# Second expert with seven block products for two of three token groups, and a planner that prices a shared port

## The chip, the cores and the metric

The kernel runs on one core of a Trainium2 chip. A core has five engines that run their own queues in order: TensorE (PE, matrix products into PSUM banks; PEld is its weight load), VectorE (DVE), ScalarE (ACT), GpSimd (POOL) and SyncE (SP, which starts DMAs). The metric is the device time of one execution in microseconds (us).

## The reference

Attention over 2 batches, 8 heads, 768 positions and head size 64, with a local window, a few global keys and a distance bias, then two feed-forward blocks on 1536 tokens of width 512:

```python
x = _attn_ref(q, k, v, n_global, n_local)   # as (1536, 512)
h = x @ moe_w_in                             # 512 x 2048
x = (h * sigmoid(h)) @ moe_w_out             # 2048 x 512
gate = sigmoid(x @ moe2_w_gate)              # 512 x 1536
val = x @ moe2_w_val                         # 512 x 1536
out = (gate * val) @ moe2_w_out              # 1536 x 512, result in float32
```

The weights arrive as 64-bit floats and are turned into 32-bit ones on the chip.

## The kernel before

Tokens are held feature-first, in three groups of 512 (`X[g]`). Every value of the two feed-forward blocks is kept as a high and a low half in TensorE's reduced fp32 format, and a product is three matmuls: high by high, high by low, low by high. All matmuls of the second block are 128 x 128 weights by 128 x 512 values.

A weight tile is 128 x 512 (512 KB in DRAM). `split_w` makes it from a staged load: one ScalarE op and three VectorE ops to reach 32 bits (`to_f32`), then one ScalarE op for the high half and one VectorE op for the low half. `pump_w` starts a load or a split every few units of work. There are 24 slots for finished tiles.

The program has two parts that are recorded and then reordered. The first is the attention, mixed with the first expert's front part. The second (`phase_rest`) runs tasks (phase, group, chunk of 128 hidden columns): `H` computes the hidden products, `act1`/`act2` apply the nonlinearity, `Y` multiplies by the output weights. In the second expert (phases B1 and B2, six chunks each, three groups) `H` makes a gate product and a val product, 12 matmuls each (4 slices of 128 input features, 3 matmuls each), and `Y` 12 more: 36 matmuls for a group and chunk, 1296 in all. Output sums stay in four PSUM banks over six chunks; `evac` then reads them once.

`Issue.order` sets the order on every engine: it walks over the recorded operations and always takes the one that can start first by its own price list (`Op.cost`, `SEM`, `TURN`), the earlier recorded where two are within 0.02. The instructions are issued in that order, and all of them carry line 257 in the profile, since one helper issues them. `nc`'s filler matmuls (line 1194, tile `warm`) stand where the planner sees room at the start. Names: `w` are weight tiles, `u` and `stage` their 32-bit form and raw load, `sg` and `g` a nonlinearity's value and its halves, `acc` the sums of a group, `x` the group's values, `t`, `pt`, `kt`, `ssum` and `nm_all` tiles of the attention.

Of the kernel before, what the change touches and what calls it, by code (L numbers as in the profile page):

```python
# [24 lines left out]
HA = 8  # L25
SLOTS = sum(r[-1] for r in PLAN)
NEG = 1.0e30
# [5 lines left out]
class Op:  # L33
# [20 lines left out]
    def cost(self):  # L54
        n = self.n
        self.form, self.half = None, 0
# [12 lines left out]
        elif self.eng == "vector":  # L69
# [3 lines left out]
            if self.meth == "tensor_scalar" and not psum and self.outs[0].name[0] == "t" and n > 64:  # L73
                self.occ += 0.1 + n / 1920.0
            self.lat = self.occ + 0.083
            self.locks = not psum and n > 128 and self.meth in ("tensor_tensor", "scalar_tensor_tensor")
        elif self.eng == "scalar":
            far = self.meth == "activation" and list(self.kw["in_"].ap)[-1][0] != 1
            slow = n > 256 and self.meth == "activation" and self.kw["in_"].space != PSUM
            self.occ = 0.045 + n / (960.0 if far else 1080.0 if slow else 1170.0) + (0.23 if "accum_out" in self.kw else 0.0)  # L80
            self.lat = self.occ + 0.1
        else:
            self.occ = n / 420.0 if self.meth == "tensor_tensor" and n > 256 else 0.13 + n / 790.0
            self.lat = self.occ + 0.03
# [20 lines left out]
def meets(x, y):  # L105
    if x[2] >= y[3] or y[2] >= x[3]:
# [6 lines left out]
        "rc": 0.195, "cr": 0.147, "tf": -0.082}  # L113


class Issue:


    def __init__(self, tc, nc):
        self.tc, self.nc, self.ops, self.on, self.open = tc, nc, [], False, None  # L120
        self.first, self.last, self.form, self.dq, self.filling = 0, {}, "f", 0.0, True
        self.lane, self.dve, self.busy = [0.0, 0.0], [], {}
        self.free, self.stop_fill = {e: 0.5 for e in SEM}, False
# [40 lines left out]
    def order(self, filler):  # L164
# [25 lines left out]
        while any(cand.values()):  # L190
            best = None
            for e, cs in cand.items():
                if cs:
                    at = [(max(free[e], max(max(m.ready, held(m)) for m in g)), p, i, g) for p, i, g in cs]
# [17 lines left out]
            for o in g:  # L212
# [9 lines left out]
                elif e == "gpsimd" and o.meth != "dma_start":  # L222
                    end = o.start + o.occ
                    for a, b in self.dve[-8:]:
                        if a < end and b > o.start:
                            end += b - max(a, o.start)
                    free[e] = end
                    o.lat = end - o.start + 0.03
# [5 lines left out]
                if e == "vector" and o.locks:  # L234
                    self.dve.append((o.start, free[e]))
# [26 lines left out]
class Engine:  # L262
# [3 lines left out]
    def __getattr__(self, meth):  # L266
        real = getattr(getattr(self.issue.nc, self.name), meth)

        def call(*args, **kw):
# [5 lines left out]
            o.stop_fill = iss.stop_fill  # L275
# [13 lines left out]
def attn_moe_moe2_kernel(  # L289
# [51 lines left out]
    clock = [0]  # L341

# [40 lines left out]
    halves2 = [range(0, C2 // 2), range(C2 // 2, C2)]  # L383
# [6 lines left out]
    for hh in halves2:  # L390
        for c in hh:
            add_w(("gate", c), colw(moe2_w_gate, c))
            add_w(("val", c), colw(moe2_w_val, c))
            add_w(("o2", c), roww(moe2_w_out, c))
# [3 lines left out]
    wtime = {}  # L398

    def wtile(key):  # L400
        return W[wid[key] % 24]

    def slot_free(n):
        if n < 16:
            return True
        if n < 24:
            return len(W) == 24
        return wfree[n - 24] >= 0
# [13 lines left out]
    def split_w(n):  # L422
        w = W[n % 24]
        st = next(u_r)
        to_f32(st, stages.pop(n))
        en.scalar.activation(out=w[:, 0, :], in_=st, func=AF.Copy)
        en.vector.tensor_tensor(w[:, 1, :], st, w[:, 0, :].bitcast(F32), ALU.subtract)

# [6 lines left out]
    def dma_w(n):  # L435
        st = next(stage_r)
# [4 lines left out]
    def pump_w():  # L441
# [3 lines left out]
        if n < wst["dma"] and clock[0] >= wtime[n] + wst["wait"] and clock[0] >= wst["last"] + wst["gap"]:  # L445
# [4 lines left out]
        if n < len(wsrc) and n - wst["split"] < 3 and slot_free(n):  # L450
# [3 lines left out]
    def need_w(key):  # L454
        n = wid[key]
        while wst["split"] <= n:
            m = wst["split"]
            if m >= wst["dma"]:
                assert slot_free(m)
                dma_w(m)  # L460
                wst["dma"] = m + 1
            split_w(m)
# [360 lines left out]
    def act2(tag, pg, pv):  # L823
        gt = next(g_r)
        g_t[tag] = gt
        sg = next(e_r)
        gf = sg
        en.scalar.activation(out=sg, in_=pg, func=AF.Sigmoid)

        def rest():  # L830
            en.vector.tensor_tensor(gf, sg, pv, ALU.mult)
            en.scalar.activation(out=gt[:, 0, :], in_=gf, func=AF.Copy)
            en.vector.tensor_tensor(gt[:, 1, :], gf, gt[:, 0, :].bitcast(F32), ALU.subtract)

        defer(4, rest)

# [94 lines left out]
    def phase_rest(prev):  # L931
        tasks = [("A1", NG - 1, c) for c in halves1[0]]
        tasks += [("A2", g, c) for g in range(NG) for c in halves1[1]]
        tasks += [("B1", g, c) for g in range(NG) for c in halves2[0]]
        tasks += [("B2", g, c) for g in range(NG) for c in halves2[1]]
        accs = acc + [main2["acc2"]]
        hi_ = [0]
# [3 lines left out]
        def H(ti):  # L941
            ph, g, c = tasks[ti]
            if ph[0] == "A":
                ps = bank[hi_[0] % 2]
                hi_[0] += 1
                for u in h_units(g, ("in", c), ps):
                    u()
                    unit()
                act1((ph, g, c), ps, False)
            else:  # L950
                pp = []
                for nm_ in ("gate", "val"):
                    ps = bank[hi_[0] % 4]
                    hi_[0] += 1
                    pp.append(ps)
                    for u in h_units(g, (nm_, c), ps):
                        u()
                        unit()
                act2((ph, g, c), pp[0], pp[1])

        def Y(ti):
            ph, g, c = tasks[ti]
            if ph[0] == "A":
                half, key, ring = halves1[0 if ph == "A1" else 1], ("out", c), [2, 3, 4, 5, 6, 7]
            else:
                half, key, ring = halves2[0 if ph == "B1" else 1], ("o2", c), [4, 5, 6, 7]
            first, last = c == half[0], c == half[-1]
            need_w(key)
            w = wtile(key)
            gt = g_t.pop((ph, g, c))  # L970
            if first:
                ybk["y"] = [bank[ring[(yrot[0] + d) % len(ring)]] for d in range(4)]
                yrot[0] += 4
            yb = ybk["y"]
            for d in range(4):
                sl = slice(d * 128, (d + 1) * 128)
                for a, b in ((0, 0), (0, 1), (1, 0)):
                    st = first and (a, b) == (0, 0)
                    fin = last and (a, b) == (1, 0)
                    if ph[0] == "A":  # L980
                        en.tensor.matmul(yb[d], w[:, a, sl], gt[:, b, :], start=st, stop=fin)
                    else:
                        en.tensor.matmul(yb[d], gt[:, a, sl], w[:, b, :], start=st, stop=fin)
                if last:
                    evac(ph, g, d, yb[d], accs[g])
                if d == 3 and g == NG - 1:
                    done_w(key)
                unit()

        def evac(ph, g, d, ps, ac):  # L990
            a = ac[:, d, :]
            if ph in ("A1", "B1"):
                en.vector.tensor_copy(a, ps)
            elif ph == "A2":
                en.vector.tensor_tensor(a, a, ps, ALU.add)
                en.scalar.activation(out=X[g][:, 0, d, :], in_=a, func=AF.Copy, scale=0.5)
                en.vector.scalar_tensor_tensor(
# [269 lines left out]
```

## Time and profile before

| | |
|---|---|
| median of 3 runs | 665.22 us (663.75 to 665.49) |
| the profiled execution | 663.89 us, its span 662.1 us |
| busy, share of the span | PE 98%, PEld 81%, DVE 56%, ACT 42%, POOL 13% |
| attention and start of the first expert | 0 to about 150 us |
| second expert | the last 1296 matmuls |
| end of PE | 655.6 us |

The busy share of PE alone doesn't say that it is at its peak, since matmuls overlap; what bounds a stretch is read from the waits and from how far apart matmuls start.

### The profile page before, as it was taken

How to read it: one execution, taken by the hardware profiler on the slowest of the kernel's cores; microseconds unless marked ns; L12 is line 12 of the kernel's file. 1: busy time of each engine (PE TensorE's matmuls, PEld its weight loads, DVE VectorE, ACT ScalarE, POOL GpSimd, SP SyncE). 2: the span in 40 equal slices, each digit the busy share in tenths (PEclk: the TensorE clock that was granted, in tenths of full speed). 3: DMA queues.
4: the chain of work that ended last, by engine and by line, in shares of the span. 5: the costliest groups of instructions: out<-in, count | busy, mean ns of one | idle time of the engine just before them, and what ended most of it. 6: DMA issues, size and time to landing. Idle time of an engine off the chain costs nothing.

```text
span 662.1 us, 9324 instructions
## 1 busy us (share of the span) xinstructions
PE 647.1 (98%) x3433; PEld 535.6 (81%) x3433; DVE 373.2 (56%) x869; ACT 277.2 (42%) x594; POOL 83.4 (13%) x167
## 2 busy tenths in 40 slices
PE   8799999999999999999999999999999999999996
PEld 6598888887888888888888888888888888888884
DVE  6999985555389999342799811312892212212212
ACT  4898787664346655222556411112452111111110
POOL 4355445333200000000000000000000000000000
PEclk9999999999999999999999999999999999999999
DMA  8757653001035545000145400000330000100101
GB/s 216 200 148 206 166 139 82 19 18 34 0 90 169 187 143 180 28 0 1 33 149 174 147 9 0 1 1 0 105 118 1 0 1 4 61 1 19 46 1 68
DMA packets 65301, 49.05 MB, mean 74 GB/s; under 512 B 39648, under 2 KB 60128, under 8 KB 65248
## 3 DMA queue, kind: packets, MB, share of 16 engines
q1 hardware_dynamic: 64032, 48.11, 25.1%
q8 instruction: 29, 0.48, 0.3%
q10 hardware_dynamic: 1216, 0.26, 0.2%
q14 instruction: 24, 0.20, 0.1%
HBM read 45.22 MB, written 3.15 MB: 73 GB/s over the span
## 4 chain that ended last, share of the span: by engine, by line
PE 86%; DVE 10%; issue 1%; ACT 1%; DMA 1%; POOL 0%; DVEq 0%; POOLq 0%
PE bank L257 86%; DVE u L257 3%; DVE t L257 2%; DVE acc L257 1%; DVE w L257 1%; ACT t L257 1%; DMA nraw<-in_n_local_dram 1%; DVE ssum L257 1%; DVE x L257 0%; DVE kt L257 0%; DVE sg L257 0%; ACT u L257 0%; DVE nm_all L257 0%; POOL t L257 0%; ACT pt L257 0%
## 5 line engine op out<-in xcount | busy, mean ns | idle before, releaser
L257 PE MATMUL bank<-x,w 128*128 128x512 f32 (+1 forms) x1488 | 349.1, 384 | 0.0
L257 PEld LDWEIGHTS bank<-x,w 128*128 128x128 f32 x1488 | 272.7, 188 | 53.5 <-issue 0.5
L257 PE MATMUL bank<-g,w 128*128 128x512 f32 (+1 forms) x624 | 145.0, 377 | 0.4 <-DVE acc L257 0.4
L257 PEld LDWEIGHTS bank<-g,w 128*128 128x128 f32 x624 | 110.7, 188 | 22.7 <-DVE acc L257 0.8
L257 ACT ACTIVATE sg<-bank 128x512 f32<-128x512 f32 x84 | 49.9, 595 | 158.7 <-PE bank L257 158.0
L257 DVE TENSOR_TENSOR sg<-sg,bank 128x512 f32<-128x512 f32 x36 | 24.7, 686 | 161.8 <-PE bank L257 161.8
L257 PE MATMUL bank<-w,g 128*128 128x512 f32 x432 | 103.4, 389 | 0.0
L257 ACT ACTIVATE g<-sg 128x512 fp32r<-128x512 f32 x84 | 53.1, 632 | 108.0 <-DVE sg L257 107.9
L257 DVE SCALAR_TENSOR_TENSOR u<-stage,u 128x512 int32<-128x512 int32 x136 | 95.0, 705 | 1.7
L257 PEld LDWEIGHTS bank<-w,g 128*128 128x128 f32 x432 | 81.1, 188 | 16.8
L257 DVE TENSOR_TENSOR g<-sg,g 128x512 fp32r<-128x512 f32 x68 | 46.8, 689 | 24.2 <-ACT g L257 23.7
L257 ACT ACTIVATE u<-stage 128x512 f32<-128x512 f32 x68 | 45.9, 676 | 32.8 <-DVE w L257 24.3
L257 ACT ACTIVATE w<-u 128x512 fp32r<-128x512 f32 x68 | 42.7, 630 | 32.5 <-DVE u L257 17.5
L257 POOL TENSOR_SCALAR t<-t,ssum 128x256 f32<-128x256 f32 (+1 forms) x88 | 48.6, 567 | 38.3 <-DVE ssum L257 35.0
L257 DVE SCALAR_TENSOR_TENSOR sg<-sg,bank 128x512 f32<-128x512 f32 x48 | 32.6, 681 | 36.6 <-ACT sg L257 36.6
L257 DVE TENSOR_TENSOR w<-u,w 128x512 fp32r<-128x512 f32 x68 | 46.7, 692 | 10.9 <-ACT w L257 10.7
L257 ACT ACTIVATE t<-t,nm_all 128x256 f32<-128x256 f32 (+1 forms) x96 | 45.8, 480 | 11.6 <-DVE nm_all L257 7.9
L257 DVE TENSOR_TENSOR acc<-acc,bank 128x512 f32<-128x512 f32 x48 | 32.1, 684 | 18.7 <-PE bank L257 18.6
L257 DVE CUSTOM_DVE_ANT_0 t<-bank,mask 128x256 f32<-128x256 f32 (+1 forms) x96 | 33.8, 393 | 5.9 <-PE bank L257 4.7
L257 DVE TENSOR_SCALAR u<-u 128x512 int32<-128x512 int32 x68 | 28.8, 426 | 4.2 <-ACT u L257 3.2
L257 ACT ACTIVATE pt<-bank 128x512 f32<-128x512 f32 (+1 forms) x48 | 26.0, 556 | 9.5 <-PE bank L257 9.3
L257 PE MATMUL bank<-ident,t 128*128 128x128 f32 x176 | 27.4, 277 | 2.3 <-POOL t L257 2.0
(68 smaller groups left out, 302.4 us busy)
## 6 DMA issues: line engine op xcount, KB each, us to landing
stage<-in_moe_w_out_dram SPq DMA_DIRECT2D x28, 512.0 KB, 3.5
stage<-in_moe_w_in_dram SPq DMA_DIRECT2D x16, 512.0 KB, 3.9
stage<-in_moe_w_gate_dram SPq DMA_DIRECT2D x12, 512.0 KB, 3.4
stage<-in_moe_w_val_dram SPq DMA_DIRECT2D x12, 512.0 KB, 3.6
v<-in_v_dram SPq DMA_DIRECT2D x12, 256.0 KB, 3.4
out_dram<-acc SPq DMA_DIRECT2D x12, 256.0 KB, 3.0
qk<-in_k_dram SPq DMA_DIRECT2D x11, 256.0 KB, 3.7
qk<-in_q_dram SPq DMA_DIRECT2D x11, 256.0 KB, 5.7
```

The costliest lines, as they stand in the source:

```text
L257: getattr(getattr(self.nc, o.eng), o.meth)(*o.args, **o.kw)
```

## The change

In the second expert chunks are taken in pairs, and groups 0 and 1 together. The input features are cut in two halves, so each of gate and val is, for a pair, a product of two 2 x 2 block matrices. These eight block products (6 matmuls each) become seven, after the scheme with seven products and fifteen block sums: four sums of value blocks (`X[1]`'s first half is overwritten by one; the others are `T2`, `T3`, `T4`), made once by GpSimd, ScalarE and VectorE when group 1 of the first expert is done; four sums of weight blocks for each pair and each of gate and val, made in `split` on VectorE (128 x 256 each), which fill two more weight tiles that ScalarE and VectorE halve; and sums of products, made by VectorE while it reads PSUM. Group 2 keeps plain products (`plain`). The output products (`down`) no longer stay in PSUM over six chunks: each pair gives a tile of 6 matmuls that ScalarE copies (first pair) or VectorE adds to `acc`, with banks 6 and 7 in turn.

Weight tiles have 16 slots in place of 24; in the second expert 12 of them serve tiles and four (4 to 7) the block sums. The price list: VectorE's tensor ops over 64 elements in SBUF now close a port shared with GpSimd, each of the two waits for the other in the plan, and `split` operations of the second expert are planned 0.5 later than they could start.

```diff
+SLACK = 0.5
...
-            if self.meth == "tensor_scalar" and not psum and self.outs[0].name[0] == "t" and n > 64:
-                self.occ += 0.1 + n / 1920.0
...
-            self.locks = not psum and n > 128 and self.meth in ("tensor_tensor", "scalar_tensor_tensor")
+            self.locks = not psum and n > 64 and self.meth != "tensor_reduce"
...
+            o.ready += o.slack
...
+        def shut(o, at):
+            a, b = self.port["gpsimd"]
+            return b if o.locks and a <= at < b else at
...
+                    a, b = self.port["vector"]
+                    got = max(o.start, b - 0.13) if a <= o.start < b else o.start
+                    free[e] = got + o.occ
...
+    loop2 = [0, 1, 2, 3, 8, 9, 10, 11, 12, 13, 14, 15]
+    slots += [loop2[n % 12] for n in range(len(wsrc) - NW1)]
...
+    SUMS = {"gate": (4, 5), "val": (6, 7)}
...
+        due = sums_due(n)
+        if due is not None:
+            a, b = ulast[0], st
+            le, ri = slice(0, 256), slice(256, 512)
+            en.vector.tensor_tensor(b[:, ri], b[:, le], b[:, ri], ALU.add)
+            en.vector.tensor_tensor(b[:, le], a[:, le], b[:, le], ALU.subtract)
+            en.vector.tensor_tensor(a[:, le], b[:, ri], a[:, le], ALU.subtract)
+            en.vector.tensor_tensor(a[:, ri], a[:, ri], a[:, le], ALU.subtract)
+            for f, sl in zip((b, a), SUMS[due[0]]):
+                en.scalar.activation(out=W[sl][:, 0, :], in_=f, func=AF.Copy)
+                en.vector.tensor_tensor(W[sl][:, 1, :], f, W[sl][:, 0, :].bitcast(F32), ALU.subtract)
...
+            if d < 2:
+                en.gpsimd.tensor_tensor(t, a, acc[0][:, d, :], ALU.subtract)
+                halved(lambda h: X[1][:, h, d, :], t)
             else:
...
+                en.gpsimd.tensor_tensor(t, a, t, ALU.subtract)
+                halved(lambda h: main2["T2"][:, h, j, :], t)
...
+        def product(ps, lhs, col, rhs, kk, start):
+            for j in range(2):
+                with en.together():
+                    for i, (a, b) in enumerate(((0, 0), (0, 1), (1, 0))):
+                        en.tensor.matmul(
+                            ps, lhs[:, a, col + j * 128:col + (j + 1) * 128], rhs[:, b, kk + j, :],
+                            start=start and j == 0 and i == 0, stop=j == 1 and i == 2, skip_group_check=not start,
+                        )
+                yield unit()
...
+            for i in range(2):
+                yield from product(bs[i][0], w[i][0], 0, X[0], 0, True)
+                en.scalar.activation(out=tc_[i], in_=bs[i][0], func=AF.Copy)
+            for i in range(2):
+                yield from product(bs[i][1], s[i][1], 0, T2, 0, True)
+                add(tu[i], tc_[i], bs[i][1])
+            for i in range(2):
+                yield from product(bs[i][2], s[i][0], 256, X[1], 0, True)
+            for i in range(2):
+                yield from product(bs[i][1], s[i][0], 0, T3, 0, False)
+                add(tv[i], tc_[i], bs[i][1])
+                add(tv[i], tv[i], bs[i][2])
...
+            for i in range(2):
+                yield from product(bs[i][1], w[i][1], 256, T4, 0, False)
+                add(tc_[i], tc_[i], bs[i][1])
...
+                yield from product(bs[i][2], s[i][1], 256, X[1], 2, False)
+                add(tu[i], tu[i], bs[i][2])
...
+                yield from product(bs[i][0], w[i][0], 256, X[0], 2, False)
...
+                a = accs[g][:, t, :]
+                if p == 0:
+                    en.scalar.activation(out=a, in_=yb, func=AF.Copy)
+                else:
+                    en.vector.tensor_tensor(a, a, yb, ALU.add)
```

Three places of the program show what moved. First TensorE in the second expert: before, two chunks of group 1 between output products (banks 2, 3, 0, 1 take gate and val; banks 4 to 7 the output sums).

```order
L257 MATMUL bank2_66<-x1_76,w11_94 128x512 x12
L257 MATMUL bank3_67<-x1_76,w12_95 128x512 x12
L257 MATMUL bank4_68<-w10_93,g2_106 128x512 x3
L257 MATMUL bank5_69<-w10_93,g2_106 128x512 x3
L257 MATMUL bank6_70<-w10_93,g2_106 128x512 x3
L257 MATMUL bank7_71<-w10_93,g2_106 128x512 x3
L257 MATMUL bank0_64<-x1_76,w14_97 128x512 x12
L257 MATMUL bank1_65<-x1_76,w15_98 128x512 x12
```

TensorE after, the end of the fourth pair's block products (banks 0 to 2 gate, 3 to 5 val; w4 to w7 are sums of weight blocks), then group 2's plain products.

```order
L260 MATMUL bank2_66<-x1_76,w4_87 128x512 x6
L260 MATMUL bank5_69<-x1_76,w6_89 128x512 x6
L260 MATMUL bank1_65<-t3_2064,w4_87 128x512 x6
L260 MATMUL bank4_68<-t3_2064,w6_89 128x512 x6
L260 MATMUL bank1_65<-t4_2065,w11_94 128x512 x6
L260 MATMUL bank4_68<-t4_2065,w13_96 128x512 x6
L260 MATMUL bank2_66<-x1_76,w5_88 128x512 x6
L260 MATMUL bank5_69<-x1_76,w7_90 128x512 x6
L260 MATMUL bank0_64<-x0_75,w10_93 128x512 x6
L260 MATMUL bank3_67<-x0_75,w12_95 128x512 x6
L260 MATMUL bank1_65<-x2_77,w10_93 128x512 x12
L260 MATMUL bank4_68<-x2_77,w12_95 128x512 x12
```

Runs of 12 matmuls into one bank became runs of 6, and a bank is written again after 6 matmuls into another one. Second, VectorE where output tiles are read: before, the sums of group 1 in the last phase.

```order
L257 TENSOR_TENSOR sg0_108<-sg0_108,bank1_65 128x512
L257 TENSOR_TENSOR acc1_79<-acc1_79,bank4_68 128x512
L257 TENSOR_TENSOR acc1_79<-acc1_79,bank5_69 128x512
L257 TENSOR_TENSOR g2_106<-sg0_108,g2_106 128x512
L257 TENSOR_TENSOR acc1_79<-acc1_79,bank6_70 128x512
L257 TENSOR_TENSOR acc1_79<-acc1_79,bank7_71 128x512
```

VectorE after, the third pair's output tiles of group 0 and the first of group 1 (`stage2` is the 32-bit form of the next weight tiles, in halves).

```order
L260 TENSOR_TENSOR acc0_78<-acc0_78,bank6_70 128x512
L260 SCALAR_TENSOR_TENSOR stage2_101<-stage0_99,stage2_101 128x512
L260 TENSOR_TENSOR acc0_78<-acc0_78,bank7_71 128x512
L260 SCALAR_TENSOR_TENSOR stage2_101<-stage0_99,stage2_101 128x512
L260 TENSOR_SCALAR stage2_101<-stage2_101 128x512
L260 TENSOR_TENSOR acc0_78<-acc0_78,bank6_70 128x512
L260 SCALAR_TENSOR_TENSOR stage2_101<-stage1_100,stage2_101 128x512
L260 TENSOR_TENSOR acc0_78<-acc0_78,bank7_71 128x512
L260 TENSOR_TENSOR g3_107<-sg0_108,g3_107 128x512
L260 TENSOR_TENSOR g2_106<-m3_2069,g2_106 128x512
L260 TENSOR_TENSOR acc1_79<-acc1_79,bank6_70 128x512
```

The reads of four banks stood together once in six chunks; now two banks alternate in every pair, and one to two operations of other work stand between two reads. Third, VectorE early in the attention (the first weight tile's low half `w0`, scores `t`, and group 0's low half `x0`): before.

```order
L257 TENSOR_TENSOR w0_83<-u0_102,w0_83 128x512
L257 ISA t4_137,nm_all_80<-bank0_64,mask0_113 128x256
L257 ISA nm_all_80 128x1
L257 TENSOR_TENSOR x0_75<-bank3_67,x0_75 128x4x128
L257 ISA t4_137,nm_all_80<-bank1_65,mask1_114 128x256
L257 ISA nm_all_80 128x1
```

The same place after.

```order
L260 ISA t4_137,nm_all_80<-bank0_64,mask0_113 128x256
L260 ISA nm_all_80 128x1
L260 TENSOR_TENSOR w0_83<-u0_102,w0_83 128x512
L260 ISA t4_137,nm_all_80<-bank1_65,mask1_114 128x256
L260 ISA nm_all_80 128x1
L260 ISA t0_133,nm_all_80<-bank0_64,mask0_113 128x256
L260 ISA nm_all_80 128x1
L260 TENSOR_TENSOR x0_75<-bank3_67,x0_75 128x4x128
```

Single operations changed places with neighbours; the same operations are there.

## Rows read from the trace of the kernel before

**Rows 1.** The page: span, and busy time of the engines.
```profile
span 662.1 us, 9324 instructions
PE 647.1 (98%) x3433; PEld 535.6 (81%) x3433; DVE 373.2 (56%) x869; ACT 277.2 (42%) x594; POOL 83.4 (13%) x167
```

**Rows 2.** The chain that ended last: start us, us, what.
```profile
86.46 59.70 PE bank L257 x433
...
152.87 500.68 PE bank L257 x2237
653.58 2.73 DVE acc L257 x4
```

**Rows 3.** All waits of TensorE: us in total, times, longest us.
```profile
PE bank L257 <- DVE x L257: 2.1, 4, 0.7
PE bank L257 <- POOL t L257: 2.0, 2, 1.9
PE bank L257 <- ACT kt L257: 1.8, 2, 1.4
...
PE bank L257 <- DVE acc L257: 0.4, 1, 0.4
```

**Rows 4.** Busy time by stretch (columns: length, engines busy, granted clock, DMA share, GB/s).
```profile
20.00:40.00 20.00, 16.32 (x149) 13.46 (x147) 19.49 (x65) 17.78 (x48) 8.07 (x17) 1.00 0.75 192
...
80.00:100.00 20.00, 19.82 (x162) 16.18 (x161) 17.73 (x69) 16.45 (x54) 10.23 (x20) 1.00 0.57 148
...
200.00:260.00 60.00, 60.00 (x266) 49.67 (x266) 59.06 (x106) 37.79 (x62) 0.00 (x0) 1.00 0.56 172
360.00:460.00 100.00, 100.00 (x443) 82.81 (x442) 33.95 (x55) 21.95 (x36) 0.00 (x0) 1.00 0.11 33
```

**Rows 5.** TensorE in order of time in the second expert: start us, us, what.
```profile
399.74 5.60 PE L257 MATMUL bank<-x,w 128*128 128x512 f32 x24
405.18 2.88 PE L257 MATMUL bank<-w,g 128*128 128x512 f32 x12
407.90 5.60 PE L257 MATMUL bank<-x,w 128*128 128x512 f32 x24
```

**Rows 6.** VectorE in order of time where it is full.
```profile
220.35 0.68 DVE L257 TENSOR_TENSOR g<-sg,g 128x512 fp32r<-128x512 f32 x1
220.96 0.42 DVE L257 TENSOR_SCALAR u<-u 128x512 int32<-128x512 int32 x1
...
222.02 0.42 DVE L257 TENSOR_SCALAR u<-u 128x512 int32<-128x512 int32 x1
222.35 2.01 DVE L257 SCALAR_TENSOR_TENSOR u<-stage,u 128x512 int32<-128x512 int32 x3
224.28 0.68 DVE L257 SCALAR_TENSOR_TENSOR sg<-sg,bank 128x512 f32<-128x512 f32 x1
```

**Rows 7.** VectorE and TensorE in order of time in the attention.
```profile
28.16 0.42 DVE L257 CUSTOM_DVE_ANT_0 t<-bank,mask 128x256 f32<-128x256 f32 x1
...
28.50 0.42 DVE L257 CUSTOM_DVE_ANT_0 t<-bank,mask 128x256 f32<-128x256 f32 x1
...
32.01 0.67 DVE L257 TENSOR_TENSOR x<-bank,x 128x512 fp32r<-128x512 f32 x1
...
32.74 0.44 PE L257 MATMUL bank<-ident,qk 128*128 128x128 f32 x2 [0.43 <-DVE x L257]
```

**Rows 8.** Costliest groups: mean ns of one ahead of the last bar.
```profile
L257 PE MATMUL bank<-w,g 128*128 128x512 f32 x432 | 103.4, 389 | 0.0
L257 ACT ACTIVATE u<-stage 128x512 f32<-128x512 f32 x68 | 45.9, 676 | 32.8 <-DVE w L257 24.3
L257 POOL TENSOR_TENSOR g<-sg,g 128x512 fp32r<-128x512 f32 x16 | 20.8, 1305 | 49.4 <-ACT g L257 42.0 <-issue 7.4
```

**Rows 9.** The end, in order of time.
```profile
647.26 8.32 PE L257 MATMUL bank<-w,g 128*128 128x512 f32 x36
...
653.58 2.73 DVE L257 TENSOR_TENSOR acc<-acc,bank 128x512 f32<-128x512 f32 x4 [3.97 <-PE bank L257]
654.33 2.34 SPq L257 DMA_DIRECT2D out_dram<-acc  x4
```

**Rows 10.** DMA issues: KB each, us to landing.
```profile
stage<-in_moe_w_val_dram SPq DMA_DIRECT2D x12, 512.0 KB, 3.6
```

More of the change, by code (lines that the diff above doesn't have):

```diff
@@ L222, in order @@
                 elif e == "gpsimd" and o.meth != "dma_start":
[L223 to L228, printed above, removed]
+                    a, b = self.port["vector"]
+                    got = max(o.start, b - 0.13) if a <= o.start < b else o.start
+                    free[e] = got + o.occ
+                    o.lat = free[e] - o.start + 0.03
+                    self.port[e] = got, free[e]
                 else:
@@ L233, in order @@
                     self.busy.setdefault(b, {})[e] = o.end
-                if e == "vector" and o.locks:
-                    self.dve.append((o.start, free[e]))
+                if o.locks:
+                    self.port[e] = o.start, free[e]
                 if o.meth == "dma_start":
@@ L341, in attn_moe_moe2_kernel @@
     clock = [0]
+    u_all, st_all = [next(u_r) for _ in range(2)], [next(stage_r) for _ in range(3)]
+    half2 = st_all[2].rearrange("p f t -> p (f t)").bitcast(F32)
+    u_all += [half2[:, 0:512], half2[:, 512:1024]]
     def run_due():
@@ L422, in split_w, with split @@
     def split_w(n):
-        w = W[n % 24]
-        st = next(u_r)
+        en.slack = SLACK if n >= NW1 else 0.0
+        split(n)
+        en.slack = 0.0
+    def split(n):
+        w = W[slots[n]]
+        st = next(u_r) if n < NW1 else u_all[n % 4]
         to_f32(st, stages.pop(n))
@@ L444, in pump_w @@
         n = wst["split"]
-        if n < wst["dma"] and clock[0] >= wtime[n] + wst["wait"] and clock[0] >= wst["last"] + wst["gap"]:
+        due = n < wst["dma"] and clock[0] >= wtime[n] + wst["wait"] and clock[0] >= wst["last"] + wst["gap"]
+        if due and can_split(n):
             split_w(n)
@@ L449, in pump_w @@
         n = wst["dma"]
-        if n < len(wsrc) and n - wst["split"] < 3 and slot_free(n):
+        if n < len(wsrc) and n - wst["split"] < (3 if n < NW1 else 2) and slot_free(n):
             dma_w(n)
@@ L941, in H @@
         def H(ti):
[L942 to L959, printed above, removed]
-        def Y(ti):
[L962 to L966, printed above, removed]
+            g, c = tasks[ti]
+            ps = bank[ti % 2]
+            for u in h_units(g, ("in", c), ps):
+                u()
+                unit()
+            act1((g, c), ps, False)
+        def Y(ti):
+            g, c = tasks[ti]
+            half = halves1[c >= HA]
             first, last = c == half[0], c == half[-1]
+            key = ("out", c)
             need_w(key)
             w = wtile(key)
-            gt = g_t.pop((ph, g, c))
+            gt = g_t.pop((g, c))
             if first:
-                ybk["y"] = [bank[ring[(yrot[0] + d) % len(ring)]] for d in range(4)]
+                ybk["y"] = [bank[(2, 5, 6, 7, 3, 4)[(yrot[0] + d) % 6]] for d in range(4)]
                 yrot[0] += 4
@@ L975, in Y @@
             for d in range(4):
[L976 to L983, printed above, removed]
+                mm3(yb[d], w, (slice(d * 128, (d + 1) * 128),), gt, (slice(0, G),), first, last)
@@ L1222, in attn_moe_moe2_kernel @@
         main2["acc2"] = late.tile([128, 4, 512], F32, name="acc2")
-        for n in range(16, 24):
-            W.append(late.tile([128, 2, 512], F32R, name=f"w{n}"))
+        for nm_ in ("T2", "T3", "T4"):
+            main2[nm_] = late.tile([128, 2, 2, 512], F32R, name=nm_.lower())
+        main2["M"] = [late.tile([128, 512], F32, name=f"m{i}") for i in range(5)] + [next(e_r), next(e_r)]
         wst["gap"] = 7
```

198 lines of the change are left out of this document (143 added, 55 removed).

## The prediction

> **What bounds the kernel now.** I read the page's first part, then the chain that ended last, then TensorE's waits, then the table by stretch. The page gives TensorE 98% of the span and VectorE 56% [rows 1], which alone proves little. The chain says more: but for a few us, all from 86 us to the end is TensorE's own matmuls, one piece of it 500.7 us with 2237 of them [rows 2]. TensorE's waits in the whole program come to about 7 us in the rows shown, nearly all in the attention, and its only wait for a sum of an expert is 0.4 us [rows 3]. From 200 to 260 us VectorE is busy 59.06 of 60.00 us and TensorE still 60.00 of 60.00, at granted clock 1.00 [rows 4]: a full VectorE costs TensorE nothing there, because nothing that TensorE needs soon stands behind it. In the second expert (360 to 460 us) VectorE has 34 of 100 us [rows 4]. So the second expert lasts as long as its matmuls take, and one matmul fewer is one less on the path, as long as VectorE and ScalarE keep up.
>
> What one matmul is worth: a period of 24 gate and val matmuls and 12 output matmuls runs from 399.74 to 407.90 us [rows 5], 8.16 us for 36, so 0.2267 us each, start to start. The mean duration of a record, 0.389 us [rows 8], contains 0.16 us in which the next already runs, and must not be multiplied.
>
> **The matmuls.** Before, a pair of chunks takes 2 x 3 groups x 36 = 216 matmuls. After, 7 block products x 6 matmuls for gate and as many for val make 84, group 2's plain products 2 x 24 = 48, the output products 3 groups x 4 tiles x 6 = 72: 204. Twelve fewer in each of six pairs are 72, and 72 x 0.2267 = 16.3 us. Attention and first expert keep theirs; two small filler matmuls more stand at the start, where TensorE has room. Forms are the same (128 x 128 by 128 x 512), so I keep 0.2267.
>
> **What VectorE gets.** Start to start, a 512-wide operation is 0.60 us (three in a row in 2.01 us, the next from 224.28) and a one-input one 0.34 (222.02 to 222.35) [rows 6]. The 256-wide two-input operation of the weight sums isn't in the trace: the nearest rows are the 256-wide scores, 0.34 apart (28.16, 28.50) [rows 7], and the 512-wide 0.60; I take 0.34, the same width, and 0.60 as the upper end. From one pair's first sum of products to the next pair's, the order after has 66, 77, 71, 70 and 51 VectorE instructions; with these prices 35.7, 41.3, 39.0, 38.4 and 29.0 us, against 204 x 0.2267 = 46.2 us of TensorE. At 0.60 for the narrow ones the fullest gets 12 x 0.26 = 3.1 us more, 44.4. So VectorE goes from a third to 77 to 90%, but isn't the longer of the two. ScalarE has 30 to 44 operations in a cycle, at most 0.68 us each [rows 8], 30 us: covered. GpSimd's eight new subtractions, 1.3 us each [rows 8], 10.4 us, lie beside group 2's part of the first expert, 192 matmuls or 43.5 us: covered, and if they were not, the first products with T2 would wait by what is left over.
>
> The duration of a 512-wide operation is 0.68 us in the rows while the next starts after 0.60 [rows 6]. The Trainium skill, "VectorE: DVE Perf Modes", section "The DRAIN you can't avoid", states that the next operation doesn't start until the pipeline is empty, though it allows an earlier start where nothing holds it. By the first half of that rule the fullest cycle would be priced with full durations, 58 wide operations at 0.68 and 19 narrow ones at 0.42, 47.4 us against TensorE's 46.2, and the sum would be 1.2 us higher; the trace bears out the second half, and I use starts.
>
> **What TensorE newly waits for.** The total fits, but not every bank does. Before, output sums are read once in six chunks, from four banks; after, tile by tile from banks 6 and 7 in turn, so that a bank is written again after six matmuls. The same holds inside a pair where a block product adds onto bank 1 or 4, which VectorE must have read first. How much time a read has: from the start of a tile's last matmul to the next start into that bank are 7 x 0.2267 = 1.59 us. It needs 0.39 for that matmul to end [rows 8], 0.04 to VectorE's start (matmul 27 of the last 36 starts at 647.26 + 26 x 0.2267 = 653.15, ends 653.54, VectorE starts 653.58 [rows 9]), 0.69 for the read (four that start 0.68 apart take 2.73 [rows 9]), and 0.06 until TensorE starts (VectorE ends 32.68, TensorE starts 32.74 [rows 7]): 1.18. So 0.41 us are left for what stands ahead in VectorE's queue. In a pair eight reads are this tight: six output tiles (the third to eighth wait for the first to sixth) and two block products; 48 in all.
>
> I laid the order of the third pair's tiles of group 0 along these numbers, tile ends 1.36 us apart. Reads start 0.20, 1.56, 3.10, 4.30 and 6.10 us after the first tile's sixth slot; the fifth tile could start at 4.08 and has its bank from 3.85. So the tightest has 0.23 us to spare, and no wait follows. The same in the fourth pair, where three matmuls of the next pair stand between tiles. Lower end: 0. Upper end: every one of the 48 finds a whole foreign operation ahead, 0.60 - 0.41 = 0.19 each, 9.1 us. A gain below 0 isn't there, since these waits don't exist now. I take one in ten late by this, 0.9 us, near the lower end, because the order written out shows none and the planner's matmul price, 0.0133 + 512/2400 = 0.2267, is what the trace shows.
>
> **Weights.** Sixteen slots in place of 24 mean that a pair's weight sums can be written only after the pair before has used its own. From that product (gate and val) until the next pair's first use, 12 + 48 + 48 = 108 matmuls follow, 24.5 us. The sums and four splits need 13.7 us of VectorE, its other work there 10.9: 24.6. That is just even, but the first two splits don't depend on it and stand earlier in the order; no wait, and 0.1 us a pair if they did. A load takes 3.6 us to land [rows 10], six in 46 us: hidden.
>
> **The attention.** The new port prices only swap neighbours there: at every eighth score the counts of splits, sums and groups done on VectorE before it are the same within one. TensorE's waits of that part, 2.1 for VectorE, 2.0 for GpSimd and 1.8 for ScalarE [rows 3], bound it: -2.0 if the wait for GpSimd goes, +2.0 if one like it comes. I take 0, since the counts agree.
>
> **The end.** The last read starts when TensorE ends (about 655.6 us) and the last DMA follows [rows 9]. After, output tiles come 1.36 us apart in place of 0.68, but the last read and last DMA stand equally far behind the last matmul: 0.
>
> **Sum**, in the profiled execution's own time: 663.89 - 16.3 + 0.9 = 648.5 us. The median of the runs shown is 665.22, which is 1.3 above; in its terms 649.8. I put the forecast between, 649.0.
>
> **Rivals.** (1) VectorE becomes a partner in step: every tight read meets one foreign operation, 9.1 us in place of 0.9, 656.7. For it: VectorE's queue is in order, filled to 90%, and some of its operations wait for ScalarE at its head. Against it: the order itself leaves 0.23 us at the tightest place. By the Trainium skill's full durations (the same section) one operation would cost 0.27 there, 13.0 us in all. (2) Slower than before: two foreign operations ahead of each tight read, because a weight split at the queue's head waits for ScalarE and reads pile up behind. Price (1.20 - 0.41) x 48 = 37.9 us, 685.5. It decides from 16.3 / 48 = 0.34 us lost at each read, that is 0.75 us of other work ahead of each. Against it: between two reads stand one or two operations, and the reads themselves are what VectorE has to do next. (3) The port prices matter: 646.5 where the attention loses its wait for GpSimd, 650.5 where it gains one more. That the change doesn't do what it says is out: the order has 72 matmuls less.
>
> **Chances.** Forecast, up to 651.5 us: 0.75. (1), 651.5 to 660: 0.14. (3) beyond 1.5 us: 0.08, half to each side. (2): 0.03. The range: 645.5 (profiled sum without waits, 647.6, less 2.0 for the attention) to 655.0, which takes in half of (1)'s waits on the upper terms; about 0.15 is left out. About 0.3%, 2 us, is what a measurement of this kernel can tell from no change; only a mixture of (1) and (2) ends there. Faster 0.95, same 0.02, slower 0.03.
>
> **What the profile after would show.** 1104 matmuls `bank<-x,w` and 216 `bank<-t,w`, in place of 1392, still 0.2267 us apart; TensorE's waits for `acc` and `m` operations under 1 us each and 2 us in all; VectorE at 75 to 90% in the second expert with no stretch of 20 us at 100%; the attention ending within 2 us of now. The forecast is wrong if matmuls of the second expert stand in runs of six with gaps, if TensorE waits for `acc` reads by 0.2 us and more again and again, if the granted clock falls, or if TensorE waits for `w` tiles at the start of a pair.

## The result, and the profile after

The changed kernel takes 646.40 us (median of 4 runs, 645.89 to 647.02), the kernel before 665.03 in the runs beside it (663.75 to 665.49): ratio 0.9723, 95% interval 0.9706 to 0.9741. The forecast was 649.0 with a range of 645.5 to 655.0. The profiled execution after took 646.85 us, its span is 645.1; before it was 663.89 and 662.1. Two executions of the kernel before beside later runs were slow, at a much lower clock (930.84 us at 0.655, 813.10 at 0.753), and enter no comparison.

The page after, answering to [rows 1]: span, and busy time of the engines. VectorE goes from 56 to 73%, TensorE's share is the same.

```profile
span 645.1 us, 9387 instructions
PE 634.1 (98%) x3363; PEld 523.5 (81%) x3363; DVE 470.8 (73%) x1043; ACT 307.5 (48%) x648; POOL 93.8 (15%) x175
```

The chain that ended last, answering to [rows 2] (start us, us, what). TensorE carries the chain from 152.71 until it ends at 639.2; before, it carried it from 152.87 to 653.55 and ended at 655.6, beside VectorE's last reads.

```profile
152.71 486.48 PE bank L260 x2174
639.21 0.69 DVE acc L260
```

All waits of TensorE, answering to [rows 3] (us in total, times, longest). None lies in the second expert; the wait for GpSimd's `t` went from 2.0 to 0.4 us, that for `x` from 2.1 to 0.5, while one for VectorE's `t` rose from 0.2 to 0.8.

```profile
PE bank L260 <- ACT kt L260: 1.8, 3, 0.9
...
PE bank L260 <- DVE t L260: 0.8, 1, 0.8
PE bank L260 <- DVE x L260: 0.5, 1, 0.5
PE bank L260 <- DVE acc L260: 0.4, 1, 0.4
PE bank L260 <- POOL t L260: 0.4, 1, 0.4
```

Busy time by stretch, answering to [rows 4], with the columns of those. From 360 to 460 us VectorE is now busy 86.18 of 100 us in place of 33.95, and TensorE still 100.00 of 100.00. New is the 0.91 of granted clock from 20 to 40 us, and that VectorE is busy 17.33 us with only 21 operations from 320 to 340 us, where GpSimd runs the eight subtractions.

```profile
20.00:40.00 20.00, 17.75 (x149) 14.78 (x147) 18.89 (x62) 17.66 (x48) 7.74 (x17) 0.91 0.67 180
...
320.00:340.00 20.00, 20.00 (x90) 16.57 (x89) 17.33 (x21) 11.66 (x20) 12.16 (x8) 1.00 0.00 1
360.00:460.00 100.00, 100.00 (x443) 82.84 (x442) 86.18 (x154) 48.86 (x83) 0.00 (x0) 1.00 0.27 81
```

A busy TensorE can still hide stalls: a matmul's record lasts 0.39 us and the next starts after 0.2267, so a stall below 0.16 us leaves no idle time. The sharper reading is how far apart the pairs start. The products with `t` tiles (`T2`, `T3`) come once in a pair; TensorE's rows of these, after:

```profile
369.61 5.60 PE L260 MATMUL bank<-t,w 128*128 128x512 f32 x24
...
415.85 4.24 PE L260 MATMUL bank<-t,w 128*128 128x512 f32 x18
...
462.09 5.60 PE L260 MATMUL bank<-t,w 128*128 128x512 f32 x24
...
508.33 5.60 PE L260 MATMUL bank<-t,w 128*128 128x512 f32 x24
...
554.57 5.60 PE L260 MATMUL bank<-t,w 128*128 128x512 f32 x24
...
600.87 5.60 PE L260 MATMUL bank<-t,w 128*128 128x512 f32 x24
```

The first five start 46.24 us apart, and 204 x 0.2267 = 46.24: the handovers between VectorE and TensorE cost 0.0 us there. The sixth starts 46.30 after the fifth, so 0.06 is lost once.

The other signs that the prediction named: its counts hold (1104 `x,w` and 216 `t,w` matmuls of 128x512), no stretch of 20 us in the second expert has VectorE over 18.71 us busy, and no wait is for a `w` tile. One sign of being wrong did show: the granted clock fell, but for 4 us in the attention and not in the second expert (last section).

### The profile page after: what moved, and what is told of

The parts are those of the page before. It is cut to its first block, busy times and chain, and to the rows that moved or that the text cites. A ratio compares the mean times of both kernels' runs of the same rounds, so it can differ in the third digit from the quotient of the medians.

```text
span 645.1 us, 9387 instructions
## 1 busy us (share of the span) xinstructions
PE 634.1 (98%) x3363; PEld 523.5 (81%) x3363; DVE 470.8 (73%) x1043; ACT 307.5 (48%) x648; POOL 93.8 (15%) x175
## 4 chain that ended last, share of the span: by engine, by line
PE 90%; DVE 6%; ACT 2%; issue 1%; POOL 1%; ACTq 0%; DVEq 0%
PE bank L260 89%; DVE u L260 2%; DVE t L260 1%; PE bank L1334 1%; DVE w L260 1%; POOL t L260 1%; ACT t L260 1%; DVE x L260 0%; DVE acc L260 0%; ACT kt L260 0%; DVE sg L260 0%; ACT u L260 0%; DVE ssum L260 0%; ACT pt L260 0%; DVE nm_all L260 0%
## 5 line engine op out<-in xcount | busy, mean ns | idle before, releaser
L260 PE MATMUL bank<-x,w 128*128 128x512 f32 (+1 forms) x1200 | 283.9, 383 | 0.0
L260 PEld LDWEIGHTS bank<-x,w 128*128 128x128 f32 x1200 | 218.4, 188 | 42.1 <-issue 0.5
L260 DVE TENSOR_TENSOR acc<-acc,bank 128x512 f32<-128x512 f32 x96 | 65.2, 684 | 31.2 <-PE bank L260 30.3
L260 DVE SCALAR_TENSOR_TENSOR u<-stage,u 128x512 int32<-128x512 int32 x100 | 69.2, 696 | 0.9
L260 ACT ACTIVATE g<-sg 128x512 fp32r<-128x512 f32 x60 | 37.9, 632 | 43.3 <-DVE sg L260 24.8
L260 PE MATMUL bank<-t,w 128*128 128x512 f32 x216 | 54.0, 389 | 0.0
L260 PEld LDWEIGHTS bank<-t,w 128*128 128x128 f32 x216 | 40.6, 188 | 8.4
L260 DVE TENSOR_TENSOR m<-m,bank 128x512 f32<-128x512 f32 x48 | 32.4, 683 | 17.0 <-PE bank L260 16.6
L260 DVE TENSOR_TENSOR g<-sg,g 128x512 fp32r<-128x512 f32 x44 | 31.0, 705 | 9.2 <-ACT g L260 7.8
L260 ACT ACTIVATE w<-stage 128x512 fp32r<-128x512 f32 x30 | 18.7, 628 | 32.0 <-DVE stage L260 19.9
```

Source lines behind the costliest of these rows:

```text
L260: getattr(getattr(self.nc, o.eng), o.meth)(*o.args, **o.kw)
```

## The experiments

Medians in us; "against" is the ratio to the kernel before as it ran beside them, with its interval. The kernel before was at 664.75, 664.39 and 664.79 beside runs 1 to 4, 5 to 8 and 9 to 11.

| run | what | median | against before |
|---|---|---|---|
| 1 | changed kernel, eight plain products for seven | 663.19 | 0.9975 (0.9964 to 0.9986) |
| 2 | changed kernel, old price list | 651.96 | 0.9804 (0.9790 to 0.9818) |
| 3 | kernel before, new price list alone | 663.40 | 0.9976 (0.9966 to 0.9986) |
| 4 | kernel before, last output tiles one by one | 663.74 | 0.9987 (0.9978 to 0.9996) |
| 5 | changed kernel, output tiles read twice | 649.43 | 0.9771 (0.9755 to 0.9786) |
| 6 | the same, read three times | 657.64 | 0.9894 (0.9878 to 0.9910) |
| 7 | changed kernel, no delay of splits | 647.89 | 0.9753 (0.9739 to 0.9767) |
| 8 | old price list, subtractions on VectorE | 648.48 | 0.9763 (0.9749 to 0.9777) |
| 9 | changed kernel again | 646.66 | 0.9723 (0.9709 to 0.9737) |
| 10 | run 7 again beside run 9 | 647.76 | 0.9741 (0.9727 to 0.9755) |
| 11 | new price list, subtractions on VectorE | 647.41 | 0.9740 (0.9725 to 0.9754) |

**1. Is it the number of matmuls?**

```diff
-                yield from product(bs[i][1], s[i][1], 0, T2, 0, True)
...
+            for g in (1, 0):
+                for j in (1, 0):
+                    for nm_, ps in (("gate", bank[k % 3]), ("val", bank[3 + k % 3])):
+                        for u in h_units(g, (nm_, 2 * p + j), ps):
```

> The changed kernel, but groups 0 and 1 take eight plain products for each pair of chunks (72 matmuls more, no block sums of weights or values); pairs, tile-by-tile output sums, sixteen slots and the new price list stay. Theory (the matmuls alone): 72 x 0.2267 = 16.3 us above the changed kernel's 646.4, so 662.7, within 1 us, TensorE without waits in the second expert. Rival (the new structure or the price list gave part of it): no more than 14 above, under 660.5. Rival (the block sums cost something that hides in the result): over 17.5 above, over 664.

It took 663.19, 16.8 above the changed kernel: nearly the whole gain goes when the 72 matmuls return, and 1.6 of 665 stay. The chain of run 1:

```profile
152.23 503.37 PE bank L260 x2246
```

Run 4 below, whose last tiles also come one by one, needs 502.72 us for as many matmuls. The 0.65 more of run 1 are handovers: its pairs of 216 matmuls start 48.97, 49.14, 49.16, 49.14 and 49.02 us apart, where 216 x 0.2267 = 48.96. TensorE's waits show none of them. So the step's size is read cleaner from run 4.

**2 and 3. The price list, taken back alone and made alone.**

```diff
-            self.locks = not psum and n > 64 and self.meth != "tensor_reduce"
+            self.locks = not psum and n > 128 and self.meth in ("tensor_tensor", "scalar_tensor_tensor")
...
-            a, b = self.port["gpsimd"]
-            return b if o.locks and a <= at < b else at
```

> The changed kernel planned with the old price list (port prices, costs and turn of before; the 0.5 of the weight splits stays). Theory (prices only swap neighbours): 646.4, within 1.5 us either way. Rival (the port prices shortened the attention): 648.5 or more, the attention ending 2 us later or more, with a wait of TensorE for GpSimd of about 2 us as in the kernel before.

> The kernel before, planned with the new price list and nothing else of the change. Theory (prices only swap neighbours): 665.0, within 1.5 us. Rival (the port prices shortened the attention): 663 or less, the last 1296 matmuls as they were and the attention shorter by 2 us.

Both runs swap the whole list: besides the port also the prices of some operations of GpSimd and VectorE and of one change of form on TensorE. Which of these moved the attention was not parted.

Run 3 is 1.35 us below the kernel before (interval 0.9 to 2.3), a number that its first theory's 1.5 us still takes in; the trace speaks for the rival: its attention ends earlier, at 151.38 in place of 152.87 in the chain, and of TensorE's waits that for `x` falls from 2.1 to 0.2 us, that for GpSimd's `t` from 2.0 to 1.6. The waits of run 3:

```profile
PE bank L259 <- POOL t L259: 1.6, 2, 1.3
...
PE bank L259 <- DVE x L259: 0.2, 1, 0.2
```

Run 2 lost 5.6 us, more than the attention can explain. TensorE's rows of run 2 at the second expert's start (idle time before a row in brackets) show where the rest is:

```profile
370.23 1.66 PE L259 MATMUL bank<-x,w 128*128 128x512 f32 x6 [2.14 <-DVE acc L259]
372.63 1.65 PE L259 MATMUL bank<-x,w 128*128 128x512 f32 x6 [0.73 <-DVE acc L259]
374.11 2.90 PE L259 MATMUL bank<-t,w 128*128 128x512 f32 x12
377.61 3.44 PE L259 MATMUL bank<-t,w 128*128 128x512 f32 x12 [0.60 <-DVE m L259]
```

And VectorE's rows of run 2 ahead of that:

```profile
365.14 0.42 DVE L259 TENSOR_TENSOR stage<-stage 128x256 f32<-128x256 f32 x1
367.61 0.43 DVE L259 TENSOR_SCALAR u<-u 128x512 int32<-128x512 int32 x1 [2.05 <-ACT u L259]
367.96 0.68 DVE L259 SCALAR_TENSOR_TENSOR u<-stage,u 128x512 int32<-128x512 int32 x1
...
369.49 0.68 DVE L259 TENSOR_TENSOR acc<-acc,bank 128x512 f32<-128x512 f32 x1
```

VectorE stands idle 2.05 us before a step of a weight split whose load (val) came later than the plan had it, and the `acc` read that TensorE needs stands behind it in the queue. Followed back, the chain of run 2 goes through that load (started at 361.43) and the gate load before it (351.57), each of which started 0.07 us after a step of VectorE on an earlier split, to VectorE from 322 us on. There VectorE's operations took up to 1.8 us in place of 0.68 beside GpSimd's subtractions:

```profile
327.42 3.48 DVE L259 SCALAR_TENSOR_TENSOR x<-acc,x 128x512 fp32r<-128x512 f32 x2
...
333.34 1.77 DVE L259 TENSOR_TENSOR w<-u,w 128x512 fp32r<-128x512 f32 x1
...
336.58 1.78 DVE L259 TENSOR_TENSOR w<-stage,w 128x512 fp32r<-128x512 f32 x1
```

The old list makes GpSimd wait for VectorE in the plan but never VectorE for GpSimd, so it planned these splits, and what follows them, too early. This was tested by runs 8 and 11.

**8 and 11. The same subtractions on VectorE, with either list.**

```diff
-                en.gpsimd.tensor_tensor(t, a, acc[0][:, d, :], ALU.subtract)
+                en.vector.tensor_tensor(t, a, acc[0][:, d, :], ALU.subtract)
```

(and the three lines like it)

> The changed kernel with the old price list, and the eight subtractions for the value sums on VectorE in place of GpSimd. With the old list alone it took 651.96, 5.6 above the changed kernel. Theory P (VectorE held up at the second expert's start, since GpSimd's subtractions use what both share): the loss there goes, only the attention's 1.4 stays: 647.8 within 1, TensorE without a gap from 360 to 380 us, VectorE's operations there 0.7 us each again. Rival (the old list spoils that place through the order alone, whoever subtracts): 651 to 653, gaps of TensorE at 370 to 380 us as with the old list.

> The changed kernel with its own price list, the eight subtractions on VectorE in place of GpSimd. With the old list this move was worth 3.5 us. Theory P (the new list already places GpSimd's subtractions where VectorE can bear them): nothing to win, 646.4 within 0.7. Rival (GpSimd's subtractions still cost VectorE time that TensorE feels): 1 us or more below. VectorE's operations between 320 and 340 us take 0.7 us each and not 1.2 to 1.8.

With the old list the move is worth 3.5 us (651.96 to 648.48), TensorE has no gap from 360 to 380 us (20.00 of 20.00), and its `t` products there start at 370.60, 1.0 later than after. So the loss comes with GpSimd's hold on VectorE where the plan takes it for nothing. The hold by itself costs TensorE nothing: in the kernel after VectorE is held as well (17.33 us for 21 operations, above), and the last val load starts no sooner (361.85 against run 2's 361.43), but the order of the new list puts the steps of both val splits behind the reads, from 370.71 on. Run 8's order differs from run 2's at this place too, so the two runs don't part the hold from the order that it spoils. With the new list there is nothing to win: 647.41, 0.75 above run 9. VectorE's operations from 320 to 340 us take 0.7 us each again in both runs. TensorE's row of run 8 shows what the move costs: here, where the first expert's products wait for a read of their bank behind VectorE's subtractions, some 0.7 us of the 1.0 arise; run 11 has the same wait:

```profile
335.11 3.01 PE L259 MATMUL bank<-x,w 128*128 128x512 f32 x12 [0.49 <-DVE sg L259]
```

**4. The end.** The kernel before, with the last two chunks of the last group multiplied tile by tile, so that the four sums are ready 1.36 us apart in place of 0.68.

```diff
+        def tail(left):
+            for d in range(4):
+                for ti in left:
...
+                evac("B2", g, d, ybk["y"][d], accs[g])
...
-            Y(ti)
+        tail(range(done, n))
```

> The kernel before, with the last two chunks of group 2 multiplied tile by tile, so that the last four output tiles come 1.36 us apart as in the changed kernel, in place of 0.68. Theory of the prediction (the last read and DMA stand equally far behind the last matmul): 665.0, no change. Rival (four DMAs at once cost the last one): the span ends 0.5 us sooner behind the last matmul (6.5 us before, 5.9 in the changed kernel), 664.5.

1.0 us below the kernel before (interval 0.3 to 1.5). The chain of run 4:

```profile
153.03 502.72 PE bank L257 x2246
655.77 0.69 DVE acc L257
```

The span ends 5.85 us behind TensorE, against 6.5 before (662.1 - 655.6) and 5.9 after (645.1 - 639.2). The difference is the last DMA itself: it starts 0.76 us behind TensorE's end in both (656.34 before, 656.49 in run 4), and lands 3.9 us later before and 3.3 in run 4, where the four stand further apart. That they get in each other's way is the likely reading; nothing else was tried. The row of the chain also gives the matmuls' price with the same kind of end: 502.72 - 486.48 = 16.24 us for 2246 - 2174 = 72.

**5 and 6. How much the handover bears.**

```diff
+                    for _ in range(1 if g < 2 else 0):
+                        en.vector.scalar_tensor_tensor(out=a, in0=yb, scalar=0.0, in1=a, op0=ALU.mult, op1=ALU.add)
```

(two in run 6)

> The changed kernel, where VectorE reads every output tile of groups 0 and 1 a second time in pairs 2 to 6 (one 512-wide operation more ahead of the bank's release; the output stays the same). 0.60 us more make the tight handover 1.18 + 0.60 = 1.78 us against 1.59, and 30 of them (6 in each of 5 pairs) are in the program. Theory A, the handover is what decides, with the sizes of the prediction: 0.19 x 30 = 5.7 us or more above the changed kernel's 646.4, so 652 to 656, with TensorE's waits for acc reads of 0.1 to 0.3 us each in the second expert, again and again. Theory B, only VectorE's total counts, and 8 more operations of 0.60 fill its fullest cycle to 46.1 of 46.2 us: 646.4, no waits.

> The same with two more reads of each tile. Theory A: handover 2.38 against 1.59 us, 0.79 x 30 = 23.7 us above the changed kernel, about 670, TensorE waiting for acc reads by 0.8 us each. Theory B (totals): VectorE's cycles 45.3, 50.9, 48.6, 48.0 and 38.6 against 46.2 us, 4.7 + 2.4 + 1.8 = 8.9 us above, about 655.

Run 5 lies between the theories, 3.0 us above the changed kernel. Its pairs start 46.24, 46.39, 46.38, 46.37 and 46.37 us apart, so they lose only 0.14 each: the planner, which knows of the second read, put three matmuls into another bank between output tiles (rows of 6 `w,g` with 3 `x,w` or `t,w` between them from 483.98 us; after, 30 and 18 `w,g` stand together). Only the last pair, where nothing is left to put between, shows theory A. Its end in the chain of run 5:

```profile
631.70 1.67 PE bank L260 x6
633.40 0.70 DVE acc L260
634.12 0.70 DVE acc L260
634.87 1.67 PE bank L260 x6
...
638.03 4.40 PE bank L260 x18
```

Two tiles in 3.17 us, 0.22 a tile more than 1.36, where 0.19 was worked out; from its first `w,g` (623.10) to TensorE's end 2.8 us are lost. Run 6, 11.2 us above, is nearer to theory B's 8.9 than to A's 23.7, but its parts are not B's. From its first `t` product (370.33) to its last 72 `w,g` matmuls (627.17) it loses 3.8 us against after (369.61 to 622.63), with VectorE busy 97.68 of 100 us from 500 to 600; and 6.9 more in the last pair, where B expected nothing, since its last tiles come every 2.04 to 2.14 us: three reads take VectorE 0.72 + 0.72 + 0.60 = 2.04. TensorE's rows of run 6 there:

```profile
627.17 2.88 PE L260 MATMUL bank<-w,g 128*128 128x512 f32 x12
630.93 1.66 PE L260 MATMUL bank<-w,g 128*128 128x512 f32 x6 [0.87 <-DVE acc L260]
632.97 1.67 PE L260 MATMUL bank<-w,g 128*128 128x512 f32 x6 [0.39 <-DVE acc L260]
635.11 1.63 PE L260 MATMUL bank<-w,g 128*128 128x512 f32 x6 [0.47 <-DVE acc L260]
...
646.19 4.37 PE L260 MATMUL bank<-w,g 128*128 128x512 f32 x18 [0.33 <-DVE acc L260]
```

**7, 9 and 10. The delay of the splits.**

```diff
-SLACK = 0.5
+SLACK = 0.0
```

> The changed kernel with the weight splits of the second expert planned without the 0.5 of delay (SLACK = 0.0). Theory A: the 0.41 us that a tight handover leaves, 0.23 at the tightest place, are enough in either order: 646.4 within 1 us, no wait of TensorE in the second expert. Rival: the delay is what keeps splits out of the way of reads; without it single reads stand behind one operation more, 0.2 to 0.6 us each, 5 to 20 times: 648 to 655 with waits for acc or m operations.

> The changed kernel again, beside the next two on the same chip, so that differences of 1 to 2 us can be told: 646.4 within 0.7, first sum products of a pair (24 matmuls on t tiles) 46.24 us apart, which is 204 x 0.2267.

> The changed kernel without the delay of the splits, again, beside the changed kernel. If the 1.5 us that it took longer are its own (its pairs lasted 46.46 to 46.70 us in place of 46.24), it is 1.1 to 1.8 above the changed kernel here too; if they were the chip's, within 0.5 of it.

Theory A is wrong by a little: 647.76 against 646.66 side by side, 1.1 us more, and 1.5 in run 7. The rival's mechanism is there, at the small end of its price. The list of waits shows none of it; the start of the pairs does, 46.42 to 46.48 us apart in run 10 (46.46 to 46.70 in run 7) in place of 46.24, which run 9 shows again (46.33 the last time). VectorE's rows of run 10 in the fourth pair show how one such 0.15 us arises:

```profile
509.82 0.69 DVE L260 TENSOR_TENSOR m<-m,bank 128x512 f32<-128x512 f32 x1 [3.39 <-PE bank L260]
510.42 0.69 DVE L260 TENSOR_TENSOR w<-u,w 128x512 fp32r<-128x512 f32 x1
511.02 0.69 DVE L260 TENSOR_TENSOR m<-m,bank 128x512 f32<-128x512 f32 x1
```

After, the two reads at this place stand back to back:

```profile
509.89 1.41 DVE L260 TENSOR_TENSOR m<-m,bank 128x512 f32<-128x512 f32 x2 [2.14 <-PE bank L260]
```

Without the delay a split's step is taken between two reads, the second is 0.60 late, and the 24 `t` products last 5.76 us in place of 5.60. That is most of the 0.2 that a pair loses, and about the price worked out for one foreign operation ahead of a tight read, 0.60 - 0.41 = 0.19, measured as 0.15.

## Why the prediction was right, and where its terms were off

**The matmuls** (16.3 us): right. 16.24 us from run 4 against after, and a pair of 46.24 us. Run 1 takes the 72 matmuls back and loses 16.8, 0.65 of it by its own handovers.

**The handovers** (0.9, between 0 and 9.1): the lower end held, 0.0 in four distances of pairs and 0.06 in the fifth. Rival (1) named a real mechanism with about the right price for one operation (0.15 to 0.22 measured, 0.19 expected), but it hardly occurs in the changed kernel: operations do stand between reads, but the order with its delay of 0.5 puts them where a read has the time. It costs 1.1 us without the delay and, with it, 0.65 in run 1, not 9.1. Rival (2) didn't come near in any run: even two more reads of each tile cost 11.2 us.

**VectorE's load**: right, 86.18 of 100 us from 360 to 460, and no cycle longer than TensorE's. From pair to pair it was busy 38.2, 41.6, 40.2, 39.9 and 28.6 us (its busy time between the starts above), where 35.7, 41.3, 39.0, 38.4 and 29.0 were worked out. One reading was wrong: the three operations from 222.35 to the next at 224.28 [rows 6] are 1.93 us, 0.64 each and not 0.60, since one of them needs the result of the one ahead and starts 0.72 us after it. The price of 0.60 stands in another of these rows (220.35 to 220.96). The full durations that the Trainium skill, "VectorE: DVE Perf Modes", section "The DRAIN you can't avoid", names first would have made a pair 47.4 us, as the prediction worked out. It is 46.24. Where an operation does need the one ahead, as run 5's second read of a tile, the next start came after 0.72 us (633.40, 634.12), not 0.60; there the rule's first half fits.

**Weights**: right; no wait for `w` in the second expert.

**The end** (0): mis-sized, -0.6 in the spans and -1.0 in run 4's median. The last read and the start of the last DMA did stay where they were behind TensorE; the prediction overlooked that the last DMA takes less time when the three ahead of it start 1.36 us apart (3.3 us to landing in run 4, 3.9 before).

**The attention** (0, bounds ±2.0): mis-sized, -1.35 in run 3, from the list of prices alone. It is rival (3)'s better side, with another wait than it named: at clock 1.00, in run 3, the wait for GpSimd lost 0.4 us and that for `x` 1.9 (1.6 each in the profile after, whose clock fell). The count of operations ahead of every eighth score was a poor measure of what the swaps do: the same counts, and yet the wait for `x` nearly went. In the profiled execution after, only 0.16 of it is to be seen at 152.71, since that one ran 4 us at a lower clock (below) and the one before none. Run 11, with the same order in the attention and its clock at 1.00 throughout, gets there at 151.90, 0.97 before 152.87. The waits in the rows shown [rows 3] come to 6.3 us, not about 7, which changes nothing here.

**GpSimd's subtractions** (covered): the sentence was right for the order after, for a reason that it didn't give. It asked only if GpSimd would be done in time, not whom it holds meanwhile. VectorE lost some 6 us between 324 and 341 us in run 2 (six operations or pairs that took 0.5 to 2.2 us longer than usual), and TensorE lost 3.5 there (2.14 + 0.73 + 0.60 in its rows, 651.96 - 648.48 in the medians); the order of the new list is what makes the cover hold.

**Sum**: 16.2 + 1.35 + 1.0 = 18.6 us, and 665.03 - 646.40 = 18.6. That these agree to the tenth is luck, since the two small terms are known to 0.7 and 0.6 us either way; the profiled spans give 16.25 + 0.16 + 0.6 = 17.0. Run 1 fits as well: 1.35 + 1.0 - 0.65 = 1.7, where 1.6 stayed. The forecast's own terms make 665.03 - 16.3 + 0.9 = 649.6 of that median, 3.2 too high: 0.9 of handovers, 1.35 of attention and 1.0 of the end, all on the good side. It was set 0.6 lower, between the execution's time and the median's, and so missed by 2.6. The time of rival (3), 646.5, was hit for only a part of its reason.

## What to carry to other kernels

Where TensorE's matmuls stand without a gap, a change is worth their number times the distance of their starts, and one can check afterwards that nothing was lost by the distance between equal places of the program, which shows stalls of 0.15 us that lists of waits and busy shares hide. Here the engine that frees TensorE's banks was 86% busy without harm, because no read was pushed back by more than the time it had to spare (0.41 us as worked out); what mattered was the order in its queue, and the planner needed a price for each engine that can hold another. When work goes to an idle engine, ask not only whether it is done in time but which busy engine it holds meanwhile.

## What the runs showed of the hardware

GpSimd's subtractions (two inputs in SBUF) hold up VectorE's operations that have two inputs in SBUF, not those with one input in a bank. VectorE after, beside GpSimd:

```profile
326.98 0.69 DVE L260 SCALAR_TENSOR_TENSOR sg<-sg,bank 128x512 f32<-128x512 f32 x1 [0.98 <-ACT sg L260]
...
329.48 1.78 DVE L260 SCALAR_TENSOR_TENSOR x<-acc,x 128x512 fp32r<-128x512 f32 x1
```

GpSimd after, in the same time:

```profile
325.40 3.01 POOL L260 TENSOR_TENSOR m<-acc 128x512 f32<-128x512 f32 x2
329.10 3.31 POOL L260 TENSOR_TENSOR m<-acc,m 128x512 f32<-128x512 f32 x2 [0.69 <-ACT t L260]
```

The read of a bank takes its usual 0.69 us while GpSimd works. The other takes 1.78: counted back by 0.68 from its end it starts at 330.58, about when GpSimd's first of two ends (329.10 + 3.31 / 2 = 330.75). The Trainium skill, "SBUF — State Buffer", section "SBUF: two separate sides", calls the pair of ports that the two engines share an exclusive lock for the whole instruction; these rows agree.

In the profile after, TensorE's clock fell once, early in the attention. The profile after by 2 us (columns as above, the granted clock third from the end):

```profile
22.00:24.00 2.00, 1.06 (x10) 0.81 (x9) 2.00 (x10) 2.00 (x8) 0.83 (x1) 1.00 0.20 78
24.00:26.00 2.00, 1.24 (x10) 0.97 (x10) 1.87 (x7) 1.83 (x4) 0.77 (x1) 1.00 0.19 44
26.00:28.00 2.00, 2.00 (x12) 1.55 (x12) 1.97 (x4) 1.35 (x3) 0.44 (x1) 0.58 1.23 278
28.00:30.00 2.00, 2.00 (x16) 1.19 (x13) 1.75 (x10) 1.85 (x7) 0.50 (x3) 0.57 0.85 279
```

After 4 us in which TensorE was busy 1.06 and 1.24 of 2.00 us the clock was at 0.58 and 0.57, mostly its lower level of 1.2 GHz, until 30 us. In the profile of before it stayed at 1.00 there. Run 3 has the same order in the attention and was busy just as little, and its clock stayed at 1.00 too:

```profile
22.00:24.00 2.00, 1.06 (x10) 0.83 (x9) 2.00 (x8) 2.00 (x7) 0.96 (x2) 1.00 0.20 78
24.00:26.00 2.00, 1.24 (x10) 0.84 (x10) 1.87 (x6) 1.59 (x5) 0.64 (x1) 1.00 0.43 98
26.00:28.00 2.00, 2.00 (x22) 1.53 (x22) 1.97 (x7) 1.62 (x3) 1.12 (x4) 1.00 1.10 276
```

So these 4 us don't decide it alone. It isn't the new order's either: run 2, with the old order, was at 0.50 and 0.67 from 32 to 36 us. Among run 9's executions those with a mean clock of 0.997 took 646.66 to 646.82 us, those with 0.999 took 645.80 and 646.08: about 0.8 us, as much as 152.71 against run 11's 151.90. That is as much as the smaller terms above, and comes and goes from run to run of the same kernel. What decides it was not found.
